# Packed attention scores: the half-seen part moved to the middle columns, and the halves of P swapped

## The chip, the core and the metric

The kernel runs on one core of a Trainium2 chip. The metric is the device time of one launch in microseconds. A core has TensorE (PE, matmuls; its weight loads are shown apart as PEld), VectorE (DVE), ScalarE (ACT), GpSimd (POOL) and SyncE (SP), which run side by side and wait for each other on semaphores. PE writes to PSUM, here eight banks of 128 partitions x 512 f32.

## What is computed

Sliding-window attention with a linear bias, then a two-layer network with a squared relu. Inputs are f32.

```python
batch, n_heads, seq, head_dim = (8, 8, 576, 64)
scores = scale * np.matmul(q, k.transpose(0, 1, 3, 2))
rel = pos[:, None] - pos[None, :]
slopes = 2.0 ** (-8.0 * (np.arange(H, dtype=np.float32) + 1) / H)
bias = slopes[:, None, None] * (-np.abs(rel).astype(np.float32))[None, :, :]
mask = (rel >= 0) & (rel < window)              # window = 128
scores = np.where(mask, scores + bias[None], -1000000000.0)
attn = softmax(scores)                          # with 1e-09 added to the sum
...
x = attn @ v, as 4608 tokens x 512
h = x @ w_in            # 512 -> 2048
r = np.maximum(h, 0.0)
out = (r * r) @ w_out   # 2048 -> 512
```

(The softmax and the last step of attention are put in short form here.)

## The kernel before

**Blocks.** A sequence of 576 is cut in four blocks of 128 queries and one of 64; eight sequences give 40 blocks, numbered m. With a window of 128, a query block sees only its own keys ("part 1") and those of the block before it ("part 0"). The scores are laid out with keys on the partitions and queries along the columns. Of the previous block a query sees only the keys that come after its own place, of its own block only those up to its own place. So, with both blocks cut in half (low = 0 to 63, high = 64 to 127):

| keys (partitions) | previous block, queries low | previous block, queries high | own block, queries low | own block, queries high |
|---|---|---|---|---|
| low | seen in part | never | seen in part | seen in full |
| high | seen in full | seen in part | never | seen in part |

Two of the eight quarters are never seen. Each half of the keys needs three column groups of 64, so 192 columns hold all the scores of a head: two groups mean the same thing for both halves of the keys (previous block with low queries, own block with high queries), and a third means one thing for the low keys (own block, low queries) and another for the high keys (previous block, high queries).

**Packed blocks.** For the blocks with a previous block, 128 queries and m >= 6 (21 of the 40) the function `layout` picks the tag "Pq", and `burst` in `score` (L558 to L583) packs them in this way. Heads come in pairs: index c names a pair, `half` chooses one head of it, and the two heads lie on the lower and the upper 64 rows of PE's array. The output's partitions (low or high keys) choose the columns of the array. So four quarters of the array work at once, each 64 x 64. The list at L564 gives the matmuls of a head, as (part, first key, first query, end of queries, first column):

```python
for part, k0, q0, q1, lo in ((0, 64, 0, 128, 64), (1, 0, 0, 64, 128), (1, 0, 64, 128, 0),
                             (1, 64, 64, 128, 0), (0, 0, 0, 64, 64)):
```

That is five matmuls: high keys 128 + 64 columns, low keys 64 + 64 + 64. In the columns before, 0 to 63 hold the own block with high queries, 64 to 127 the previous block with low queries, and 128 to 191 the group with two meanings.

**After the burst.** ScalarE takes exp of the 192 columns of two heads (of one bank) into the bf16 tile `raw` (L613, four a block). VectorE multiplies by `masks` (the bias's exponential, 0 outside the window) into the tile P (L621): one cut of all 128 partitions and two heads for the two plain groups, four a block, and after every second of these two corner cuts of 64 partitions and four heads for the third group. P holds for each head 256 columns, before the change first the own block's 128 and then the previous block's 128. The two never-seen corners of P are zeroed once, at the start (L395, L396). Then `mix` multiplies P by v (L668), 16 matmuls of 65 columns a block; the 65th column is the sum of the softmax. DVE divides (L691, L696) and the result x is transposed into xT, on PE for 11 blocks and by a DMA transpose on SP (L706) for 29. kqT, the transposed keys and queries, comes in the same way (PE for 9 blocks, SP at L487 for 31).

**Other blocks.** The rest use the tag "P" with whole 64- or 128-column pieces (L579); a block of 64 queries shares a tile with the first block of the next sequence. `at_of` (L541) says where in P each part lies.

**The network.** Tokens go in nine groups g of 512. L772 multiplies xT by w_in (64 matmuls of 512 columns a group, in groups 0 and 1 of fewer columns), ACT takes the relu (L781), DVE squares (L788), and L835 multiplies by w_out.

**The order of the work.** `Plan.order` is a list scheduler. Each `plan.add` gives a task with its engine, its price in ns, a key, the tasks it depends on and the slots that it takes and frees. The planner simulates the engines and DMA rings with these prices, and the resulting start times give the order in which the instructions are written out. Prices thus have no effect but on the order, and, in the first 26 us, on how many filler matmuls on a zero tile (L875) stand in PE's planned gaps. Three prices matter here: `mm(n)`, of nearly every matmul but the score bursts, `max(n, 64) / 2.4 + 1.5`; the score bursts (L584), 220 ns and 176 for each packed unit of four heads; and the masks of L621, `dve(256, 2)` = 205 ns each.

A score burst takes three units (two when it starts early in the list), so a full packed burst has 3 x 2 pairs x 10 = 60 matmuls.

Of the kernel before, what the change touches and what calls it, by code (L numbers as in the profile page):

```python
# [12 lines left out]
ALU = mybir.AluOpType  # L13
# [230 lines left out]
def kernel(  # L244
    ctx: ExitStack, tc: tile.TileContext, q, k, v, moe_w_in, moe_w_out, out
):
    nc = tc.nc
# [41 lines left out]
    ident32 = const.tile([128, 128], FP32)  # L289
    kq32 = const.tile([128, 2, d_model], FP32)  # L290
    zero = const.tile([128, 128], BF16)
    masks = const.tile([128, H, 2, 128], BF16)
    pair_masks = const.tile([128, H, 256], BF16)
    dist = const.tile([128, 2, 128], FP32)
# [14 lines left out]
    raw = ring("raw", size["raw"], [128, H, 256])  # L309
# [8 lines left out]
    def dve(n, rate=1):  # L318
        return n / rate / 0.96 + 72.0

    def mm(n):
        return max(n, 64) / 2.4 + 1.5


    def build_iota():
        nc.gpsimd.iota(dist, pattern=[[128, 2], [1, 128]], base=0, channel_multiplier=-1,
                       allow_small_or_imprecise_dtypes=True)

    t_iota = plan.add({"POOL": 360.0}, -9e5 + 1.005, build_iota)

    def build_ident():
        nc.vector.tensor_single_scalar(ident32, dist[:, 0], 0.0, op=ALU.is_equal)

    t_ident = plan.add({"DVE": 480.0}, -9e5 - 1, build_ident, [t_iota])

# [28 lines left out]
        nc.vector.tensor_copy(pair_masks[:, :, 0:128].rearrange("p h (t s) -> p h t s", t=2), masks[:, :, :, 0:64])  # L364

    def pair_own():
        nc.vector.tensor_copy(pair_masks[:, :, 128:256], masks[:, :, 0, :])

    t_pair = [plan.add({"DVE": n}, PAIR_KEY, f, t_mask) for n, f in ((670.0, pair_rest), (960.0, pair_own))]

# [7 lines left out]
    def zero_task(o, n):  # L378
        def emit():
            nc.vector.memset(o, 0.0)  # L380
        task = plan.add({"DVE": dve(n)}, -9e5 + 9, emit, [t_ones])
        return task
# [9 lines left out]
    zero_first("kqT", kqT, lambda t: t[:, 0:C, 64:128], 128)  # L392
    t_zero_P = []
    for t in Pt["Pq"]:
        t_zero_P.append(zero_task(t[0:64, :, 1, 64:128], 512))  # L395
        t_zero_P.append(zero_task(t[64:128, :, 0, 0:64], 512))  # L396

    def warm():
        idle(bank(sw), WARM)
# [131 lines left out]
    def layout(ms):  # L531
        pair = len(ms) == 2
        quarters = not pair and ms[0] % NKB and blk[ms[0] % NKB] == 128 and ms[0] >= QUARTERS
        sP = Slot("Pq" if quarters else "P")
        work_of = []
        for i, m in enumerate(ms):
            b, kb, n, _, first = where(m)
            parts_of[m] = ([(0, m - 1)] if kb else []) + [(1, m)]
            P_of[m] = (sP, [])
            for part, mk in parts_of[m]:  # L540
                at = 64 * (1 - part) if pair and i == 0 else 128 if pair else 128 * (1 - part)  # L541
                at_of[m, part] = at
                rel = [sk_of[mk]] if part == 0 or kb == NKB - 1 else []
                work_of.append((m, mk, n, at, rel))
        for m in ms:
            P_of[m] = P_of[ms[0]]
        return ms, sP, work_of, where(ms[0])[3]

    def score(units):
# [8 lines left out]
        def burst():  # L558
            for sl in slots.values():
                bank(sl)  # L560
            for (ms, sP, work_of, _), j in units:
                for c in (2 * j, 2 * j + 1) if sP.tag == "Pq" else ():
                    m = ms[0]
                    for part, k0, q0, q1, lo in ((0, 64, 0, 128, 64), (1, 0, 0, 64, 128), (1, 0, 64, 128, 0),  # L564
                                                 (1, 64, 64, 128, 0), (0, 0, 0, 64, 64)):
                        mk = m - 1 + part
                        lo += (c % 2) * 256
                        for half in range(2):
                            rows = slice(half * 64, half * 64 + 64)
                            nc.tensor.matmul(  # L570
                                slots[m, 2 * j + half].tile[k0:k0 + 64, lo:lo + q1 - q0],
                                kqT[sk_of[mk].idx][rows, c, k0:k0 + 64], kqT[sk_of[m].idx][rows, C + c, q0:q1],
                                start=True, stop=True)
                for c in () if sP.tag == "Pq" else (2 * j, 2 * j + 1):
                    for m, mk, w, at, _ in work_of:
                        for k0 in range(0, 128, tall):
                            for half in range(2):
                                rows = slice(half * 64, half * 64 + 64)
                                nc.tensor.matmul(  # L579
                                    slots[ms[0], 2 * j + half].tile.rearrange("p (c x) -> p c x", c=2)[  # L580
                                        k0:k0 + tall, c % 2, at:at + w],
                                    kqT[sk_of[mk].idx][rows, c, k0:k0 + tall], kqT[sk_of[m].idx][rows, C + c, 0:w],
                                    start=True, stop=True)  # L583
# [3 lines left out]
                      [t for u in units for w in u[0][2] for x in w[:2] for t in t_kq_of[x]] + chain["s"],  # L587
                      [*slots.values()] + [u[0][1] for u in first_of if u[0][1].tag == "P"],
                      [x for u in units if u[1] == 1 for w in u[0][2] for x in w[4]])
        tm.n = 4 * sum(5 if u[0][1].tag == "Pq" else len(u[0][2]) * 128 // tall for u in units)  # L590
        plan.bursts.append(tm)
        chain["s"] = [tm]
        for (ms, sP, work_of, due), j in units:
            pair = len(ms) == 2
            hi = max(w[3] for w in work_of) // 128 + 1
            lo = min(w[3] for w in work_of) // 128
            n = 128 if pair else work_of[0][2]
            cols = 2 * sum(w[2] for w in work_of)

            def view(t, pair=pair, lo=lo, hi=hi, n=n):  # L600
                if pair:
                    return t
                return t.rearrange("p c (t q) -> p c t q", t=2)[:, :, lo:hi, 0:n]

            t_exp = []
            for i in (2 * j, 2 * j + 1) if sP.tag == "Pq" else ():
                slot = slots[ms[0], i]
                if i == 0:
                    raw_of[ms[0]] = Slot("raw")
                sr = raw_of[ms[0]]  # L610

                def expo(i=i, slot=slot, sr=sr):
                    nc.scalar.activation(raw[sr.idx][:, 2 * i:2 * i + 2, 0:192],  # L613
                                         slot.tile.rearrange("p (c x) -> p c x", c=2)[:, :, 0:192],
                                         AF.Exp, bias=0.0, scale=scale)
                te = plan.add({"ACT": act(384) + 50.0}, due - 28 + 3 * i, expo, [tm], [sr] if i == 0 else [], [slot])
                t_exp.append(te)

                def mask(ks, hs, lo, to, sr=sr, sP=sP):
                    P = Pt["Pq"][sP.idx].rearrange("p h t q -> p h (t q)")[ks, hs, to]  # L620
                    nc.vector.tensor_tensor(P, raw[sr.idx][ks, hs, lo], masks.rearrange("p h t q -> p h (t q)")[ks, hs, to],  # L621
                                            op=ALU.mult)
                whole, low, high = slice(0, 128), slice(0, 64), slice(64, 128)
                cuts = [(whole, slice(2 * i, 2 * i + 2), whole, slice(64, 192))]
                if i % 2:
                    four, corner = slice(2 * i - 2, 2 * i + 2), slice(128, 192)
                    cuts += [(low, four, corner, low), (high, four, corner, slice(192, 256))]
                for n, w in enumerate(cuts):
                    P_of[ms[0]][1].append(plan.add(
                        {"DVE": dve(256, 2)}, due - 28 + 3 * i, functools.partial(mask, *w),  # L630
                        t_exp[-1:] + t_exp[-2:-1] * (n > 0) + t_zero_P + t_mask,
                        [sP] if i == 0 else [], [sr]))
            for i in () if sP.tag == "Pq" else (2 * j, 2 * j + 1):
                slot = slots[ms[0], i]

                def Pv(i=i, sP=sP, view=view):
                    return view(Pt["P"][sP.idx][:, 2 * i:2 * i + 2].rearrange("p h t q -> p h (t q)"))

                def expo(i=i, Pv=Pv, view=view, slot=slot):
                    nc.scalar.activation(Pv(i), view(slot.tile.rearrange("p (c x) -> p c x", c=2)),  # L640
                                         AF.Exp, bias=0.0, scale=scale)
                te = plan.add({"ACT": act(cols) + 50.0}, due - 28 + 3 * i, expo, [tm], [], [slot])

                def mask(i=i, pair=pair, Pv=Pv, view=view):
                    pt = Pv(i)
                    mk = (pair_masks if pair else masks.rearrange("p h t q -> p h (t q)"))[:, 2 * i:2 * i + 2]
                    nc.vector.tensor_tensor(pt, pt, view(mk), op=ALU.mult)  # L647
                P_of[ms[0]][1].append(plan.add(
                    {"DVE": dve(cols, 2)}, due - 28 + 3 * i, mask,
                    [te] + (t_pair if pair else [t_mask[h] for h in range(H) if place(h) // 2 == i])))  # L650
# [282 lines left out]
```

## Time and profile before

| | |
|---|---|
| median of 7 runs | 312.58 us |
| all runs | 311.9 to 316.07 us |
| the profiled execution | 316.07 us, its span 314.3 us |
| mean granted PE clock | 0.995 |
| PE busy 26 to 80 us | 53.84 of 54.00 us |
| PE busy 244 to 297 us | 53.00 of 53.00 us |
| L613, exp of packed scores | 84 times, mean 501 ns |
| L668, P times v, packed blocks | 336 times, mean 193 ns |
| kqT transposes by DMA | 31, median 6.7 us from issue to landing |
| xT transposes by DMA | 29, median 5.5 us from issue to landing |

How to read the lines that follow. A group's line gives the line of the kernel, the engine, the operation, output <- inputs, the shape (for PE: rows x columns of the array, then rows x streamed columns), the count, then busy time in us and the mean ns of one, then the idle time of the engine ahead of them and who ended it. [...] In a line by stretch come the stretch, its length, and the busy time and count of PE, PEld, DVE, ACT and POOL, then the granted PE clock, the DMA share (here two DMA queues add up, so it can pass 1) and GB/s. A timeline line gives start and length in us; neighbours of one kind are merged.

### The profile page before, as it was taken

Reading aid. Unit: us, or ns where it says so; the run is one execution under the profiler, and the core shown is the slowest. Engines: PE = TensorE matmul, PEld = TensorE weight load, DVE = VectorE, ACT = ScalarE, POOL = GpSimd, SP = SyncE. Lnnn points to the kernel's source line nnn. Section 1 sums busy time; section 2 is a strip of 40 time slices with the busy share of each in tenths; the row PEclk is TensorE's granted clock in tenths of the full one; section 3 lists DMA queues with packets and bytes.
Section 4 is the critical chain, followed back from the end, with each engine's and each line's share of the span. In section 5 each row is a group of like instructions: output and inputs, shape, how many; then the busy total and the mean of one; then the engine's idle time right before and its main releaser. Section 6 shows DMA issues by size and latency. Waiting matters only on the chain.

```text
span 314.3 us, 8213 instructions
## 1 busy us (share of the span) xinstructions
PE 304.0 (97%) x3306; PEld 169.9 (54%) x3306; DVE 170.5 (54%) x563; ACT 171.6 (55%) x338; POOL 107.5 (34%) x134
## 2 busy tenths in 40 slices
PE   7799999999969999999999999999999999999996
PEld 3577887875535455455544554455545454444443
DVE  7774757667345884674736565466547643222200
ACT  4965776574227772774655574367356553434411
POOL 8938577445542527355613333011100000000000
PEclk9999999999997999999999999999999999999999
DMA  9999999999999999999999999998931111000022
GB/s 132 151 184 188 175 185 139 136 136 147 117 123 159 168 132 140 161 94 160 160 219 168 147 158 158 181 136 88 241 111 50 53 52 43 34 35 33 33 88 81
DMA packets 168631, 40.07 MB, mean 127 GB/s; under 512 B 159952, under 2 KB 164304, under 8 KB 168592
## 3 DMA queue, kind: packets, MB, share of 16 engines
q0 software_dynamic: 114896, 18.88, 86.7%
q1 hardware_dynamic: 53696, 20.65, 39.1%
q8 instruction: 26, 0.43, 0.6%
q14 instruction: 13, 0.11, 0.1%
HBM read 36.70 MB, written 9.44 MB: 147 GB/s over the span
## 4 chain that ended last, share of the span: by engine, by line
PE 87%; DMA 7%; POOL 3%; issue 1%; DVE 0%; SPq 0%; ACT 0%; POOLq 0%
PE A L772 39%; PE A L835 38%; PE A L668 5%; DMA w_out_sb<-in_moe_w_out_dram 4%; DMA xT<-x 3%; PE A L570 3%; POOL kq L445 2%; PE A L579 1%; POOL vt L445 1%; PE A L515 1%; PE A L714 1%; POOL w_in_sb L414 0%; SPq L487 0%; ACT kqT L464 0%; DVE Pq L621 0%
## 5 line engine op out<-in xcount | busy, mean ns | idle before, releaser
L772 PE MATMUL A<-xT,w_in_sb 128*128 128x512 bf16 (+3 forms) x768 | 147.1, 327 | 3.1 <-DMA xT<-x 2.9
L835 PE MATMUL A<-w_out_sb,g 128*128 128x512 bf16 (+2 forms) x592 | 147.7, 374 | 0.4 <-DMA w_out_sb<-in_moe_w_out_dram 0.4
L781 ACT ACTIVATE rt<-A 128x512 bf16<-128x512 f32 (+1 forms) x148 | 86.3, 591 | 94.6 <-PE A L772 83.1
L788 DVE TENSOR_TENSOR g<-rt 128x512 bf16<-128x512 bf16 (+1 forms) x148 | 60.9, 415 | 82.9 <-ACT rt L781 82.0
L772 PEld LDWEIGHTS <-w_in_sb 128*128 128x128 bf16 x768 | 68.4, 98 | 53.6 <-issue 3.7
L835 PEld LDWEIGHTS <-g 128*128 128x128 bf16 x592 | 54.2, 98 | 56.2 <-issue 0.9
L445 POOL DMA_DIRECT2D vt<-in_v_dram x40 | 33.9, 850 | 93.3 <-PE A L668 81.6
L621 DVE TENSOR_TENSOR Pq<-raw,masks 64x256 bf16<-64x256 bf16 (+1 forms) x168 | 43.5, 285 | 11.2 <-ACT raw L613 8.3
L445 POOL DMA_DIRECT2D kq<-in_k_dram x39 | 33.7, 864 | 15.8 <-DMA kqT<-kq 7.2
L613 ACT ACTIVATE raw<-A 128x384 bf16<-128x384 f32 x84 | 35.5, 501 | 6.3 <-PE A L570 6.3
L804 ACT ACTIVATE osb<-A 128x512 f32<-128x512 f32 (+1 forms) x36 | 21.5, 598 | 28.3 <-PE A L835 24.5
L445 POOL DMA_DIRECT2D kq<-in_q_dram x39 | 33.6, 861 | 7.0 <-DMA kq<-in_q_dram 2.4
L696 DVE TENSOR_TENSOR x<-A,rec 128x256 bf16<-128x256 f32 (+1 forms) x80 | 32.3, 416 | 0.8
L812 POOL DMA_DIRECT2D out_dram<-osb x3 | 1.7, 564 | 71.9 <-ACT osb L804 71.9
L640 ACT ACTIVATE P<-A 128x512 bf16<-128x512 f32 (+1 forms) x48 | 24.0, 576 | 3.0 <-PE A L579 2.9
L691 DVE RECIPROCAL rec<-A 128x4 f32<-128x4 f32 (+1 forms) x80 | 13.2, 176 | 20.6 <-PE A L668 19.8
L668 PEld LDWEIGHTS <-Pq 128*128 128x128 bf16 x336 | 15.1, 97 | 8.2 <-DVE Pq L621 0.6
L668 PE MATMUL A<-vt,Pq 128*128 128x65 bf16 x336 | 16.6, 193 | 0.2 <-DVE Pq L621 0.2
L668 PEld LDWEIGHTS <-P 128*128 128x128 bf16 x240 | 11.0, 98 | 5.7 <-DVE P L647 0.8
L647 DVE TENSOR_TENSOR P<-P,pair_masks 128x512 bf16<-128x512 bf16 x28 | 11.6, 420 | 3.7 <-ACT P L640 2.7
L570 PEld LDWEIGHTS <-kqT 64*64 64x64 bf16 x840 | 10.0, 110 | 5.6 <-issue 5.5
L668 PE MATMUL A<-vt,P 128*128 128x65 bf16 x240 | 12.1, 193 | 0.7 <-DMA vt<-in_v_dram 0.7
(43 smaller groups left out, 114.2 us busy)
## 6 DMA issues: line engine op xcount, KB each, us to landing
out_dram<-osb SPq DMA_DIRECT2D x32, 256.0 KB, 3.0
vt<-in_v_dram POOLq DMA_DIRECT2D x32, 128.0 KB, 5.7
kq<-in_k_dram POOLq DMA_DIRECT2D x31, 128.0 KB, 7.0
kq<-in_q_dram POOLq DMA_DIRECT2D x31, 128.0 KB, 7.5
w_in_sb<-in_moe_w_in_dram POOLq DMA_DIRECT2D x4, 512.0 KB, 9.0
w_out_sb<-in_moe_w_out_dram POOLq DMA_DIRECT2D x4, 512.0 KB, 10.1
out_dram<-osb POOLq DMA_DIRECT2D x3, 256.0 KB, 2.3
kq<-in_k_dram POOLq DMA_DIRECT2D x8, 64.0 KB, 8.4
```

Source lines behind the costliest of these rows:

```text
L445: nc.gpsimd.dma_start(o, src[b, :, kb * 128:kb * 128 + n, :].rearrange("h s d -> s h d"))
L570: nc.tensor.matmul(slots[m, 2 * j + half].tile[k0:k0 + 64, lo:lo + q1 - q0], kqT[sk_of[mk].idx][rows, c, k0:k0 + 64], kqT[sk_of[m].idx][ro ...
L613: nc.scalar.activation(raw[sr.idx][:, 2 * i:2 * i + 2, 0:192], slot.tile.rearrange("p (c x) -> p c x", c=2)[:, :, 0:192], AF.Exp, bias=0.0 ...
L621: nc.vector.tensor_tensor(P, raw[sr.idx][ks, hs, lo], masks.rearrange("p h t q -> p h (t q)")[ks, hs, to], op=ALU.mult)
L640: nc.scalar.activation(Pv(i), view(slot.tile.rearrange("p (c x) -> p c x", c=2)), AF.Exp, bias=0.0, scale=scale)
L668: nc.tensor.matmul(bank(slot_v)[:, hi * (D + 1):(hi + 1) * (D + 1)], Pt[sP.tag][sP.idx][:, place(h)].rearrange("p t q -> p (t q)")[:, at_o ...
L696: nc.vector.tensor_tensor(xt[sx.idx][0:n, hf * 256:(hf + 1) * 256].rearrange("p (h e) -> p h e", h=4), pv[0:n, :, 0:D], srec.tile[0:n, :]. ...
L772: nc.tensor.matmul(bank(slot)[:, fi * w:(fi + 1) * w], w_in_sb[:, cc, fc * 128:(fc + 1) * 128], xT[:, cc, g * 512 + lo:g * 512 + hi], star ...
L781: nc.scalar.activation(srt.tile[:, 0:cols], slot.tile[:, 0:cols], AF.Relu, bias=0.0, scale=1.0)
L788: nc.vector.tensor_tensor(sg.tile[:, fcs[0]:fcs[-1] + 1, lo:hi], r, r, op=ALU.mult)
L804: nc.scalar.activation(so.tile[:, lo:hi], slot.tile[:, lo:hi], AF.Copy)
L835: nc.tensor.matmul(bank(slot)[:, lo:hi], sg.tile[:, fc, t * 128:(t + 1) * 128], w_out_sb[:, fc, lo:hi], start=fc == 0, stop=fc == FCB - 1)
```

## The change

The list of matmuls has four entries. The group with two meanings moves to columns 64 to 127. With it in the middle, "own block, low queries" and "own block, high queries" are neighbours for the low keys, as the two groups of the previous block are for the high keys, so one matmul of 128 columns writes both. For that the halves of P and of `masks` are swapped: previous block first, own block second. The two plain groups are now columns 0 to 63 and 128 to 191 of `raw`, and columns 0 to 63 and 192 to 255 of P and `masks`, so the wide mask cut has two runs of 64 for each head. The mask source `dist` starts at 128 and falls, the identity and one pair mask are taken from its other half, and the zeroed corners move along. In the planner, `mm` is 0.8 ns a matmul higher, and the masks cost 205 ns (wide) and 290 ns (corners); the count of instructions in a burst goes from 5 to 4 a head. The price of a burst stays.

```diff
     def mm(n):
-        return max(n, 64) / 2.4 + 1.5
+        return max(n, 64) / 2.4 + 2.3
...
-        nc.gpsimd.iota(dist, pattern=[[128, 2], [1, 128]], base=0, channel_multiplier=-1,
+        nc.gpsimd.iota(dist, pattern=[[-128, 2], [1, 128]], base=128, channel_multiplier=-1,
...
-        nc.vector.tensor_single_scalar(ident32, dist[:, 0], 0.0, op=ALU.is_equal)
+        nc.vector.tensor_single_scalar(ident32, dist[:, 1], 0.0, op=ALU.is_equal)
...
-        nc.vector.tensor_copy(pair_masks[:, :, 128:256], masks[:, :, 0, :])
+        nc.vector.tensor_copy(pair_masks[:, :, 128:256], masks[:, :, 1, :])
...
-        t_zero_P.append(zero_task(t[0:64, :, 1, 64:128], 512))
-        t_zero_P.append(zero_task(t[64:128, :, 0, 0:64], 512))
+        t_zero_P.append(zero_task(t[0:64, :, 0, 64:128], 512))
+        t_zero_P.append(zero_task(t[64:128, :, 1, 0:64], 512))
...
-                at = 64 * (1 - part) if pair and i == 0 else 128 if pair else 128 * (1 - part)
+                at = 64 * part if pair and i == 0 else 128 * part
...
-                    for part, k0, q0, q1, lo in ((0, 64, 0, 128, 64), (1, 0, 0, 64, 128), (1, 0, 64, 128, 0),
-                                                 (1, 64, 64, 128, 0), (0, 0, 0, 64, 64)):
+                    for part, k0, q0, q1, lo in ((0, 64, 0, 128, 0), (1, 0, 0, 128, 64),
+                                                 (1, 64, 64, 128, 128), (0, 0, 0, 64, 0)):
...
-        tm.n = 4 * sum(5 if u[0][1].tag == "Pq" else len(u[0][2]) * 128 // tall for u in units)
+        tm.n = 4 * sum(4 if u[0][1].tag == "Pq" else len(u[0][2]) * 128 // tall for u in units)
...
                 def mask(ks, hs, lo, to, sr=sr, sP=sP):
-                    P = Pt["Pq"][sP.idx].rearrange("p h t q -> p h (t q)")[ks, hs, to]
-                    nc.vector.tensor_tensor(P, raw[sr.idx][ks, hs, lo], masks.rearrange("p h t q -> p h (t q)")[ks, hs, to],
-                                            op=ALU.mult)
-                whole, low, high = slice(0, 128), slice(0, 64), slice(64, 128)
-                cuts = [(whole, slice(2 * i, 2 * i + 2), whole, slice(64, 192))]
+                    P = Pt["Pq"][sP.idx].rearrange("p h t q -> p h (t q)")[ks, hs]
+                    mk = masks.rearrange("p h t q -> p h (t q)")[ks, hs]
+                    r = raw[sr.idx][ks, hs]
+                    if to is None:
+                        o, r, mk = (t.rearrange("p h (a b) -> p h a b", b=64)[:, :, 0:n:n - 1]
+                                    for t, n in ((P, 4), (r[:, :, 0:192], 3), (mk, 4)))
+                    else:
+                        o, r, mk = P[:, :, to], r[:, :, lo], mk[:, :, to]
+                    nc.vector.tensor_tensor(o, r, mk, op=ALU.mult)
+                low, high = slice(0, 64), slice(64, 128)
+                cuts = [(slice(0, 128), slice(2 * i, 2 * i + 2), None, None)]
                 if i % 2:
-                    four, corner = slice(2 * i - 2, 2 * i + 2), slice(128, 192)
-                    cuts += [(low, four, corner, low), (high, four, corner, slice(192, 256))]
+                    cuts += [(ks, slice(2 * i - 2, 2 * i + 2), high, to)
+                             for ks, to in ((low, slice(128, 192)), (high, high))]
...
-                        {"DVE": dve(256, 2)}, due - 28 + 3 * i, functools.partial(mask, *w),
+                        {"DVE": 205.0 if n == 0 else 290.0}, due - 28 + 3 * i, functools.partial(mask, *w),
```

More of the change, by code (lines that the diff above doesn't have):

```diff
@@ L594, in score @@
             pair = len(ms) == 2
-            hi = max(w[3] for w in work_of) // 128 + 1
             lo = min(w[3] for w in work_of) // 128
@@ L598, in score, with view @@
             cols = 2 * sum(w[2] for w in work_of)
-            def view(t, pair=pair, lo=lo, hi=hi, n=n):
+            def view(t, pair=pair, lo=lo, n=n):
                 if pair:
                     return t
-                return t.rearrange("p c (t q) -> p c t q", t=2)[:, :, lo:hi, 0:n]
+                return t.rearrange("p c (t q) -> p c t q", t=2)[:, :, lo:2, 0:n]
             t_exp = []
```

## The prediction

> **What bounds the kernel now.** I read the page's busy times first, then the chain that ended last, then busy time by stretch, then the waits, and last the one kind of burst that the change rewrites.
>
> ```profile
> PE 304.0 (97%) x3306; PEld 169.9 (54%) x3306; DVE 170.5 (54%) x563; ACT 171.6 (55%) x338; POOL 107.5 (34%) x134
> ...
> PE 87%; DMA 7%; POOL 3%; issue 1%; DVE 0%; SPq 0%; ACT 0%; POOLq 0%
> ```
>
> TensorE (PE) is busy for 304.0 of 314.3 us and carries 87% of the chain; VectorE (DVE) carries none of it. So time is won by giving PE less to do, or lost by making PE wait. The stretches say where it still waits (us; PE, PEld, DVE, ACT, POOL busy; granted clock):
>
> ```profile
> 0.00:26.00 26.00, 21.92 (x241) 14.62 (x242) 18.57 (x64) 16.95 (x37) 19.01 (x28) 1.00 1.53 160
> 26.00:80.00 54.00, 53.84 (x826) 41.22 (x824) 36.34 (x124) 34.22 (x71) 34.04 (x41) 1.00 1.95 155
> 80.00:90.00 10.00, 9.73 (x129) 5.10 (x127) 4.70 (x17) 3.71 (x8) 4.69 (x6) 1.00 2.12 127
> 90.00:98.00 8.00, 5.06 (x81) 2.44 (x78) 2.35 (x7) 2.69 (x6) 2.32 (x3) 0.79 1.92 130
> 98.00:170.00 72.00, 71.94 (x838) 36.91 (x837) 47.45 (x165) 45.30 (x90) 32.31 (x39) 1.00 1.80 159
> 170.00:244.00 74.00, 74.00 (x821) 37.30 (x820) 41.60 (x133) 41.35 (x81) 13.47 (x17) 1.00 1.02 138
> ```
>
> PE misses 4 us in the first 26, then nothing but one hole near 90 us. The waits name the hole:
>
> ```profile
> PE A L772 <- DMA xT<-x: 2.9, 1, 2.9
> ```
>
> One transposed tile of x landed at 92.9 us; PE waited, and its clock fell to 0.79 in that stretch. The start-to-start times of single matmuls there put the gap at 3.1 us and the slower matmuls after it at another 1.4 us or so. The profiled run took 316.07 us (span 314.3 and 1.8 around it). Without that hole it would be 316.07 - 4.5 = 311.6; the other six runs took 311.9 to 313.1. So the median run, 312.58, has at most about 1 us of this kind of wait, and I take the hole as mostly a property of the profiled run.
>
> Now the burst, groups by form and then the timeline of the burst at 136.65 us:
>
> ```profile
> L570 PE MATMUL A<-kqT 64*64 64x64 bf16 x504 | 11.2, 196 | 0.0
> L570 PE MATMUL A<-kqT,kqT 64*64 64x128 bf16 x168 | 10.5, 226 | 0.0
> L570 PE MATMUL A<-kqT,kqT 64*64 64x64 bf16 x168 | 10.2, 195 | 0.0
> L570 PEld LDWEIGHTS <-kqT 64*64 64x64 bf16 x840 | 10.0, 110 | 5.6 <-issue 5.5
> ```
> ```profile
> 136.74 0.24 PE L570 MATMUL A<-kqT,kqT 64*64 64x64 bf16 x4
> ...
> 136.84 0.23 PE L570 MATMUL A<-kqT,kqT 64*64 64x64 bf16 x4
> ...
> 136.93 0.23 PE L570 MATMUL A<-kqT,kqT 64*64 64x64 bf16 x4
> ...
> 137.36 0.39 PE L772 MATMUL A<-xT,w_in_sb 128*128 128x512 bf16 x1
> ```
>
> 840 matmuls are 21 packed blocks x 8 heads x 5. A full burst is 60 of them (6 pairs of heads, one head on each half of the array's rows). The rows "kqT,kqT 64x64" recur once a pair: 136.74, .84, .93, that is every 95 ns. In the timeline's records the burst starts at 136.652, its last matmul starts 580 ns later, the next L772 starts 125 ns after that; the L772 before it started 309 ns ahead of the burst, where two such matmuls are 216 ns apart. So a burst costs 93 + 705 = 798 ns, of which 93 and about 96 are the changes of shape at its ends, which stay.
>
> **The change part by part.**
>
> *Fewer matmuls.* 21 x 8 = 168 matmuls and their 168 weight loads go. The columns streamed don't: each half of the keys still gets 192 columns a head (before 128+64 on the high half and 64+64+64 on the low; after 128+64 on both). The single starts show what a matmul costs in its quarter of the array. Low keys: starts every 31 to 32 ns, three of them 95 ns. High keys: 59 ns after the 128-column one and 28 or 29 after the 64-column one, together 87.5. The low half with its three matmuls sets the pace; 192 columns cost 95 ns in three pieces, 87.5 in two. After the change both halves have the two-piece form, which the high half shows today, so a pair takes 87.5 ns: 7.5 x 84 pairs (21 x 4) = 0.63 us, all on PE's path. Bounds: if the new pairing doesn't reach 87.5 because both 128-column pieces now start together, the gain is 0; if the burst is paced by instructions instead (580/60 = 9.7 ns each), it is 168 x 9.7 = 1.6 us. I take 0.63, since each half's own spacing is seen directly.
>
> [...]
>
> *The wide mask cut (L621, 84 times).* It becomes two runs of 64 elements a head where it was one of 128. Today's two forms bracket it:
>
> ```profile
> L621 DVE TENSOR_TENSOR Pq<-raw,masks 64x256 bf16<-64x256 bf16 x84 | 23.7, 282 | 0.7
> L621 DVE TENSOR_TENSOR Pq<-raw,masks 128x256 bf16<-128x256 bf16 x84 | 23.0, 288 | 10.5 <-ACT raw L613 8.3
> ```
>
> By the code the first has four runs of 64 and the second two of 128; 282 and 288 ns say that shorter runs cost nothing. I take 0. [...] DVE is half idle, so what counts is how long P is ready before PE takes it. Over the 21 blocks the starts of the P matmuls lie behind the end of the masks they need by 0.06 and 0.26 us for the first four heads in the tightest two blocks, by 0.17, 0.42 and 0.44 us for the last four in the tightest three, and by 0.6 to 12.5 us in the rest. [...]
>
> *The corner cuts, zeros, iota, identity, pair masks.* Same counts and sizes at other columns: 0. The cover is that they are set-up in the first 26 us, or the same 282 ns step. ScalarE's exponentials read the same 192 columns: 0.
>
> *The planner's prices.* Every matmul is priced 0.8 ns higher (2.3 where it was 1.5 over columns/2.4), the two corner masks 290 where they were 205. The trace says that both are nearer the truth: a 512-column matmul comes every 216 ns (planned 214.8, now 215.6), and from one corner to the next corner DVE takes 288 to 291 ns. No instruction gets longer by it, but the list of all 3306 matmuls is laid out anew: by 90 us the plan is some 1080 x 0.8 = 0.9 us later, and near ties fall otherwise. Steps moved by it are the P matmuls, the x transposes on SP and the loads on POOL. What such a move can cost is bounded by the trace: at best the ~1 us of waiting in the median and part of the 4 us missing in the first 26 us; at worst one more hole like the one at 90 us, 4.5 us. I take 0, since after 98 us PE has no hole, and most xT tiles land 0.8 to 2.3 us before their first matmul, where a local shift over 10 us (46 matmuls x 0.8) is 0.04 us.
>
> Sum: on the profiled run's own time 316.07 - 0.63 = 315.4; on the median of the runs 312.58 - 0.63 = 312.0 (rounded).
>
> **The rivals.** About 0.5% (1.6 us) is what a measurement of this kernel can tell from no change: bounds 311.0 and 314.1.
>
> *Slower: the new order makes PE wait for an xT tile in every run.* At 68 to 90 us the transposes on SP take 7 to 9 us from issue to landing, and two issues held SP itself for 4.8 and 6.7 us; the tile that PE waited for had no slack. For it: that stage is already at its limit, and a kqT transpose put ahead of an xT one on SP is enough. Against it: the six other runs show at most 1 us. It decides once the tile lands over 2 us behind its matmul (2.2 in place of 0.63 gained, clock loss included). Price: the profiled run's excess, 3.5 us: 312.0 + 3.5 = 315.5.
>
> *Faster than the sum: the plan that agrees with the chip removes waits.* The remaining 1 us of xT wait and some 0.6 of the 4 us at the start go: 312.0 - 1.6 = 310.4. For it: both new prices match the trace. Against it: PE is full from 26 us on but for the hole.
>
> [...]
>
> *The change doesn't shorten the burst:* the columns are the same 192 a half; 312.6.
>
> **How the numbers follow.** Likeliest, the sum: 0.45, 311.2 to 313.0 by itself. No shorter burst, or slower masks: 0.10, within 0.5%. Faster rival: 0.21. Slower rival: 0.24. Of the sum's 0.45, 0.03 falls below 311.0 with the burst's upper bound (1.6 us), and 0.02 above 314.1 with part of a hole. Faster 0.24, same 0.50, slower 0.26. The range reaches into both rivals, 310.3 to 315.0.
>
> **What the profile after would show.** L570 with 672 matmuls, 336 of them 128 columns wide; full bursts of 48, with pairs every 87 to 88 ns and about 660 ns from first matmul to the next shape instead of 705. [...] PE busy from 98 us to 297 us without holes. The prediction is wrong if PE shows a new wait for DMA xT, kqT or vt, or if the first 26 us miss clearly more or less than 4 us of PE.

## The result and the profile after

The changed kernel takes 310.71 us (median of 27 runs) against 312.59 us (64 runs of the kernel before beside it): ratio 0.9939, 95% interval 0.9925 to 0.9953, so 1.9 us less (1.5 to 2.3). The forecast was 312.0 us, 0.6 us less, in a range of 310.3 to 315.0. The changed kernel's profiled execution took 310.01 us, with a span of 308.3.

The page's busy times, and busy time by stretch (columns as before):

```profile
PE 300.9 (98%) x3138; PEld 167.9 (54%) x3138; DVE 170.6 (55%) x563; ACT 170.9 (55%) x338; POOL 107.6 (35%) x134
```
```profile
0.00:26.00 26.00, 22.06 (x245) 14.85 (x246) 18.44 (x64) 17.37 (x38) 19.41 (x28) 1.00 1.57 163
26.00:80.00 54.00, 54.00 (x786) 41.02 (x785) 36.17 (x123) 33.60 (x70) 33.51 (x41) 1.00 2.02 157
80.00:90.00 10.00, 9.44 (x114) 4.85 (x113) 5.00 (x18) 3.71 (x8) 5.77 (x8) 1.00 2.01 136
90.00:98.00 8.00, 8.00 (x118) 4.34 (x117) 5.46 (x20) 6.27 (x13) 4.11 (x6) 1.00 2.37 153
98.00:170.00 72.00, 72.00 (x770) 36.42 (x769) 46.53 (x155) 43.42 (x85) 31.53 (x38) 1.00 1.79 161
```

168 matmuls are gone, PE is full from 26 us to 297 us but for 0.56 us ahead of 90 us, and the start misses 3.9 us as before. The 0.56 us are a wait for a tile of xT:

```profile
PE A L777 <- DMA xT<-x: 0.6, 1, 0.6
```

The burst is as forecast. By form, and in the timeline of the burst at 135.12 us (rows kept: the first matmuls of a pair, and the ends):

```profile
L570 PE MATMUL A<-kqT 64*64 64x128 bf16 x168 | 10.1, 222 | 0.0
L570 PE MATMUL A<-kqT,kqT 64*64 64x128 bf16 x168 | 10.1, 223 | 0.0
L570 PEld LDWEIGHTS <-kqT 64*64 64x64 bf16 x672 | 8.6, 108 | 5.9 <-issue 5.9
```
```profile
135.12 0.24 PE L570 MATMUL A<-kqT,kqT 64*64 64x128 bf16 x2
...
135.30 0.24 PE L570 MATMUL A<-kqT,kqT 64*64 64x64 bf16 x4
...
135.38 0.24 PE L570 MATMUL A<-kqT,kqT 64*64 64x64 bf16 x4
135.41 0.24 PE L570 MATMUL A<-kqT 64*64 64x128 bf16 x4
135.47 0.24 PE L570 MATMUL A<-kqT,kqT 64*64 64x64 bf16 x4
...
135.77 0.39 PE L777 MATMUL A<-xT,w_in_sb 128*128 128x512 bf16 x1
```

336 matmuls are 128 columns wide. The single matmuls overlap (one of 128 columns is shown with 222 ns); their starts give a pair every 87.5 ns (one and the same matmul of the six pairs starts 86, 174, 261, 349, 436 and 524 ns behind the burst's first), and 649 ns from the burst's first matmul to the next L777, where it was 705 in the burst shown before. The wide mask cut, now with two runs of 64, has not changed:

```profile
L627 DVE TENSOR_TENSOR Pq<-raw,masks 64x256 bf16<-64x256 bf16 x84 | 23.7, 282 | 0.8
L627 DVE TENSOR_TENSOR Pq<-raw,masks 128x256 bf16<-128x256 bf16 x84 | 22.4, 288 | 12.4 <-ACT raw L612 10.5
```

So 56 ns in each of 14 bursts (84 pairs, six to a burst) explain about 0.8 us. Where do the other 1.1 us come from? My first theory was the order that the new planner prices give.

### The profile page after: what moved, and what is told of

The parts are those of the page before. It is cut to its first block, busy times and chain, and to the rows that moved or that the text cites. A ratio compares the mean times of both kernels' runs of the same rounds, so it can differ in the third digit from the quotient of the medians.

```text
span 308.3 us, 7879 instructions
## 1 busy us (share of the span) xinstructions
PE 300.9 (98%) x3138; PEld 167.9 (54%) x3138; DVE 170.6 (55%) x563; ACT 170.9 (55%) x338; POOL 107.6 (35%) x134
## 4 chain that ended last, share of the span: by engine, by line
PE 89%; DMA 6%; POOL 3%; issue 0%; DVE 0%; POOLq 0%
PE A L777 40%; PE A L840 39%; PE A L673 5%; DMA w_out_sb<-in_moe_w_out_dram 4%; PE A L570 3%; DMA xT<-x 3%; POOL kq L445 2%; PE A L579 1%; POOL vt L445 1%; PE A L515 1%; PE A L719 1%; POOL w_in_sb L414 0%; POOL dist L326 0%; DVE osb L811 0%; POOLq L326 0%
## 5 line engine op out<-in xcount | busy, mean ns | idle before, releaser
L777 PE MATMUL A<-xT,w_in_sb 128*128 128x512 bf16 (+3 forms) x768 | 145.3, 326 | 0.8 <-DMA xT<-x 0.6
L777 PEld LDWEIGHTS <-w_in_sb 128*128 128x128 bf16 x768 | 68.5, 98 | 51.6 <-DMA w_in_sb<-in_moe_w_in_dram 0.7
L570 PEld LDWEIGHTS <-kqT 64*64 64x64 bf16 x672 | 8.6, 108 | 5.9 <-issue 5.9
```

The lines of the kernel that those rows point to most:

```text
L570: nc.tensor.matmul(slots[m, 2 * j + half].tile[k0:k0 + 64, lo:lo + q1 - q0], kqT[sk_of[mk].idx][rows, c, k0:k0 + 64], kqT[sk_of[m].idx][ro ...
L777: nc.tensor.matmul(bank(slot)[:, fi * w:(fi + 1) * w], w_in_sb[:, cc, fc * 128:(fc + 1) * 128], xT[:, cc, g * 512 + lo:g * 512 + hi], star ...
```

## Experiments

### The two halves of the change apart

**four_old_order**: the changed kernel with the old prices, so that every instruction outside the bursts stands in the order of before.

```diff
-        return max(n, 64) / 2.4 + 2.3
+        return max(n, 64) / 2.4 + 1.5
-        tm.n = 4 * sum(4 if u[0][1].tag == "Pq" else ...
+        tm.n = 4 * sum(5 if u[0][1].tag == "Pq" else ...
-                        {"DVE": 205.0 if n == 0 else 290.0}, ...
+                        {"DVE": dve(256, 2)}, ...
```

> Four matmuls a head and the swapped halves of P, but the planner's prices of before, so every instruction outside the bursts stands in the order of before. Theory (the burst gives 56 ns each in 14 bursts, about 0.8 us; the rest of the 1.9 us came from the order that the new prices give): 311.8 us, ratio 0.9975. Rival (the shorter burst brings all of it, since what follows it starts earlier): 310.7 us, ratio 0.994.

Measured: 310.42 us, ratio 0.9935 (0.9915 to 0.9956).

**five_new_order**: the kernel before with the new prices, the same three edits the other way round.

> The kernel before with the new prices alone (0.8 ns more a matmul, masks at 205 and 290 ns, four instructions a head counted): five matmuls a head in the order of the changed kernel. Theory (order worth 1.1 us): 311.5 us, ratio 0.9965. Rival (the burst brings all): 312.6 us, ratio 1.000.

Measured: 312.10 us, ratio 0.9982 (0.9964 to 0.9999). The theory falls: with the old order the four matmuls bring all of the gain, and the new order brings some 0.2% (0.36% at most by the interval).

**four_mm15**: the changed kernel with the old matmul price alone, a third order (`+ 2.3` to `+ 1.5`).

> The changed kernel with the matmul price of before (1.5 ns over columns/2.4), masks at 205 and 290 ns: a third order. If the nearer matmul price is what made the order better, this loses the 1.1 us: 311.8 us. If the mask price did it, 310.7 us. If it is chance which order has the waits, anything from 310.5 to 313.

Measured: 310.80 us, ratio 0.9946 (0.9931 to 0.9961). Three orders of the four-matmul kernel lie within 0.4 us. For the four-matmul kernel the prices are worth nothing that these runs can tell.

**six_new_order**: what paces a burst.

```diff
-((0, 64, 0, 128, 0), (1, 0, 0, 128, 64), (1, 64, 64, 128, 128), (0, 0, 0, 64, 0))
+((0, 64, 0, 64, 0), (1, 0, 0, 64, 64), (0, 64, 64, 128, 64), (1, 0, 64, 128, 128),
+ (1, 64, 64, 128, 128), (0, 0, 0, 64, 0))
```

> The changed kernel with both 128-column matmuls of a head cut in two, so six matmuls of 64 columns, three on each half of the keys; same prices, same order. If the fullest quarter of the array sets the pace, a pair takes 95 ns as with five matmuls, and the time is 0.8 us over the changed kernel: 311.5 us. If the number of instructions sets the pace (a pair took 95 ns with 10, 88 with 8), a pair takes 105 to 115 ns and the time is 1.5 to 2.3 us over the changed kernel: 312.2 to 313.0 us.

Measured: 312.44 us, ratio 0.9984 (0.9967 to 1.0002), so some 1.4 us over the changed kernel, between the two forecasts. The single starts of the burst at 137.02 us tell why: the second to the fifth pair begin every 95 ns (116, 211, 306, 401 ns behind the first), as three 64-column matmuls one behind the other took before (95 ns), but the sixth begins 141 ns behind the fifth; it is 634 ns from first to last start against 527. From the second to the fifth pair the pace is the quarter's; why the sixth comes later, these runs don't tell. (The profile also waits 1.0 us longer for an xT tile near 90 us than the changed kernel's, so it is not shown that the bursts, 14 times 0.107 us by this estimate, are all of the 1.4 us.)

### Where the excess lies

Four matmuls gain 1.3 to 2.0 us in two orders, and the bursts account for 0.8. New theory: PE waits less for DMA.

**five_light** and **four_light**: the kernel before, and four_old_order, with half the rows of most loads left out, so that the DMA queues have less to do and the order stays. (The rows left out hold older data, so what these two compute is no longer the attention.)

```diff
+                w = 64 if m >= 7 and m != 10 else n
-                o = (vt[sl.idx][0:n, :, 0:D] if nm == "v"
-                     else kq[sl.idx][0:n, i].rearrange("s (h d) -> s h d", h=H))
+                o = (vt[sl.idx][0:w, :, 0:D] if nm == "v"
+                     else kq[sl.idx][0:w, i].rearrange("s (h d) -> s h d", h=H))
-  ... src[b, :, kb * 128:kb * 128 + n, :] ...
+  ... src[b, :, kb * 128:kb * 128 + w, :] ...
```

> The kernel before, but for blocks from 7 on (all but block 10) only the first 64 of 128 rows of k, q and v are loaded, so those DMAs move half the bytes; the order of instructions stays. The rest of the rows hold older data. It is a pair with four_light. If the excess of the measured 1.9 us over the 0.8 us of the shorter bursts is DMA waits of PE ahead of 110 us, they vanish here: about 311.0 us, and the pair differs by 0.8 us. If the excess lies elsewhere on PE, the pair differs by 1.7 to 2.0 us.

> Four matmuls a head in the order of before (four_old_order), with the same halved loads as five_light. Excess in DMA waits: 0.8 us below five_light, about 310.2 us. Excess on PE itself: 1.7 to 2.0 us below five_light.

Measured: five_light 310.96 us, ratio 0.9949 (0.9929 to 0.9970); four_light 310.31 us, ratio 0.9928 (0.9908 to 0.9949). With light queues the pair differs by 0.65 us, close to what the bursts are worth. four_light is no faster than four_old_order (310.42), five_light is 1.5 us faster than the kernel before: the excess is a wait of the five-matmul kernel that the four-matmul kernel in this order mostly lacks, and that goes with the load on the DMA queues.

**before_look** and **before_look2**: two more profiles of the kernel before, no edit.

> The kernel before once more, for a second profile. If its usual time has DMA waits, PE shows one or more holes between 60 and 110 us that add up to about 1 us, and from the burst near 103 us to the end it takes 206.0 + 0.8 us. If the excess is on PE, the stretch from that burst to the end takes over 207.5 us.

> As before_look, a third profile of the kernel before: the same expectation, to see whether the holes stand at one place.

Measured: 312.25 and 312.53 us, usual times. From the burst at 102.8 us to the end they take 207.7 and 208.0 us, which by what I had written puts the excess on PE and not on data. Behind the first 26 us the waits of before_look2 name no DMA, but a hole ended by "issue", the profile's word for time in which the engine waited for nothing that it shows:

```profile
PE A L579 <- issue: 1.2, 1, 1.2
```

The timelines of before_look and before_look2 show it, inside one burst:

```profile
109.40 0.20 PE L579 MATMUL A<-kqT,kqT 64*64 64x64 bf16 x4
109.43 0.25 PE L579 MATMUL A<-kqT 64*64 64x64 bf16 x5
110.57 0.25 PE L579 MATMUL A<-kqT 64*64 64x128 bf16 x3 [0.89 <-issue]
```
```profile
109.43 0.25 PE L579 MATMUL A<-kqT 64*64 64x64 bf16 x5
110.85 0.25 PE L579 MATMUL A<-kqT 64*64 64x128 bf16 x3 [1.17 <-issue]
```

Both stop three matmuls ahead of the end of the burst. Counted by weight loads (each with its matmul, and PE's few waits and drains), both stop after PE's instruction 3009, and the profiled run of before had a gap of 0.3 us at 114.1 us after the same one. The page lists a DMA queue of kind "instruction":

```profile
q8 instruction: 26, 0.43, 0.6%
```

That is 26 packets of 16 KB beside PE's 6,631 instructions, 255 to a packet if the queue carries PE's, and the positions at which PE stops (below) lie 256 instructions or a multiple of that apart. So I take a packet to be a piece of 256 instructions of PE, an estimate from these counts. Packet times and positions, from the trace, in us:

```
kernel                packet near 108 us   burst begins   stops after   goes on
before_look           107.80 to 109.05     108.82         3009          110.57
before_look2          108.09 to 109.30     108.82         3009          110.85
before, profiled run  111.73 to 113.02     113.51         3009          114.43
five_new_order        109.04 to 110.36     109.33         3009          111.84
four_old_order        111.90 to 113.57     108.61         no stop       -
changed kernel        111.14 to 112.68     108.63         no stop       -
```

The packet in the table is the one that follows the piece ending at 3009. In the four traces that stop it began with 132 to 156 instructions left. Among 512-column matmuls (216 ns each) 130 instructions, 65 matmuls with their weight loads, last 14 us. A burst of 68 matmuls is 136 instructions and uses them up in 0.65 us, while PE went on only 2.7 to 2.8 us after the packet began (107.80 to 110.57). In these four the packet began 0.3 to 1.8 us ahead of the burst, and PE stood for 0.3 us (before, profiled run), 0.9 and 1.2 us (before_look, before_look2) and 1.5 us (five_new_order).

How many are left is not fixed. In before_look the packets between 47 and 110 us, with the DMA queues busy, begin with 99 to 153 left; from 250 us on, with the queues nearly idle, with 280 to 290. In five_light, with light queues and the same instructions, the packet for 3009 began at 105.79 us with 184 left and ended at 106.82, 2.2 us ahead of the burst, and PE runs through 3009. That fits the excess going with the DMA load: under load the packet came later.

The other stops fit. four_old_order stops for 0.3 us at 66.8 us and four_mm15 for 0.6 us at 67.4 us, both after instruction 1729 or 1730, five times 256 ahead of 3009; before_look for 0.3 us at 57.4 us and five_light for 0.6 us at 57.6 us, both after 1473, six times 256 ahead. So the four-matmul kernel has such stops too, but smaller ones.

One matmul in five dropped from each packed head shifts the boundary. By the burst near 109 us, four_old_order has had 136 fewer instructions (its burst begins at 2743, not 2879), and the piece that ends at 3009 ends well behind that burst (PE reaches 3009 only at 117.0 us).

### Testing the fetch theory

**five_shift30** and **four_shift140**: more instructions at the very start. The warm-up's 2560 columns of a zero tile are cut in more matmuls: 20 and 75 in place of 5.

```diff
-        idle(bank(sw), WARM)
+        for w in [128] * 20:                   # four_shift140: [32] * 70 + [64] * 5
+            nc.tensor.matmul(bank(sw)[:, 0:w], zero, zero[:, 0:w], start=True, stop=True)
```

> The kernel before with its 20 x 128 warm-up columns in 20 matmuls in place of 5: 30 more instructions ahead of everything, the same columns and the same order after. New theory: the excess over the 0.8 us is one hole of PE in the burst near 109 us, where PE runs through the last instructions of a 16 KB fetch (256 instructions) before the next fetch has come, and 30 instructions more move that fetch some 20 matmuls ahead of the burst. Then the hole goes and the time is 311.2 to 311.5 us, ratio 0.9965. Rival (DMA waits for data by chance, whatever the instruction count): 312.5 us, ratio 1.000.

> Four matmuls a head in the order of before, with the warm-up's 2560 columns in 75 matmuls in place of 5: 140 more instructions. By the fetch theory the end of a fetched piece now falls two instructions ahead of the end of the 128-instruction burst near 109 us, and its fetch starts just ahead of that burst: a hole of 1 to 1.5 us appears there, 311.4 to 312.2 us against 310.4 of four_old_order. Rival (the four-matmul burst lost the hole by being shorter, or waits are by chance): 310.4 us.

Measured: five_shift30 312.62 us, ratio 0.9998 (0.9980 to 1.0016); four_shift140 311.04 us, ratio 0.9951 (0.9929 to 0.9973). In five_shift30 the hole near 109 us is gone as forecast (the burst runs through), but the time is not: a wait of 1.1 us for an xT tile stands at 90 us.

```profile
89.72 0.41 PE L672 MATMUL A<-vt,P 128*128 128x65 bf16 x8
91.26 0.81 PE L776 MATMUL A<-xT,w_in_sb 128*128 128x512 bf16 x3 [1.14 <-DMA xT<-x]
```

The tile landed at 91.1 us, against 89.4 and 89.7 in before_look and before_look2. An instruction packet ran from 87.90 to 89.37 in this run, and only from 89.3 on in those two; whether it held up the tile is not shown. In four_shift140 the fetch began at 107.41 us, 1.6 us ahead of the burst at 109.02 and not just ahead of it, and the burst lost only 0.1 us at instruction 3009, which PE reached 1.15 us behind the packet's end. The 0.6 us over four_old_order stand in the first 33 us (0.8 us later there). The hole was placed wrongly, and the run does not decide whether a full one comes back.

**five_split** and **four_hole**: the same test, with the added instructions between the xT wait near 90 us and the burst near 109 us. Matmuls of token group 2, of the second and third of the four steps of the sum, are cut in 2 or 4 pieces.

```diff
+                    cut = {2: 4, 3: 4, 4: 2, 5: 2}.get(fc, 1) if g == 2 and cc in (1, 2) else 1
+                    # four_hole: 4 for fc 1 to 10, 2 for 11 and 12
+                    for a in range(0, w, w // cut):
+                        z = a + w // cut
-   nc.tensor.matmul(bank(slot)[:, fi * w:(fi + 1) * w], ..., xT[:, cc, g * 512 + lo:g * 512 + hi], ...)
+   nc.tensor.matmul(bank(slot)[:, fi * w + a:fi * w + z], ..., xT[:, cc, g * 512 + lo + a:g * 512 + lo + z], ...)
```

> The kernel before, with 8 of the 512-column matmuls of token group 2 (93 to 107 us) cut in pieces: 32 more instructions between the xT wait near 90 us and the burst near 109 us, 0.03 us more of PE, and every other instruction in the same order. Fetch theory: the end of the fetched piece now falls 98 instructions into that burst of 136 and its fetch starts some 40 instructions ahead of it, so the hole of 1.1 to 1.4 us goes, while the xT wait near 90 us, ahead of the edit, stays as before: 311.2 to 311.5 us, ratio 0.996 to 0.9965. Rival (another wait takes the hole's place, as with the 30 instructions at the start): 312.5 us, ratio 1.000.

> Four matmuls a head in the order of before, with 22 pairs of matmuls of the same token group cut in pieces: 128 more instructions ahead of the burst near 109 us, 0.2 us more of PE. Fetch theory: the fetch starts at the first instruction of that burst of 128, and 138 instructions are at hand, gone in about 0.8 us, so PE stands for 1.5 to 2 us behind the burst: 312.0 to 312.6 us, ratio 0.9985 to 1.000. Rival (with four matmuls there is no such hole): 310.6 us, ratio 0.994.

Measured: five_split 311.89 us, ratio 0.9976 (0.9957 to 0.9995); four_hole 312.06 us, ratio 0.9979 (0.9963 to 0.9994).

four_hole is the clear one: the hole is back, at the place that was set for it, with four matmuls a head. Its packet ran from 107.27 to 108.92, the burst began at 108.03, and PE stopped after instruction 3009:

```profile
108.62 0.26 PE L579 MATMUL A<-kqT 64*64 64x64 bf16 x8
108.82 0.33 PE L673 MATMUL A<-vt,Pq 128*128 128x65 bf16 x5
110.46 0.27 PE L673 MATMUL A<-vt,Pq 128*128 128x65 bf16 x3 [1.32 <-issue]
```

From one start to the next that is 1.51 us, 1.48 more than usual. With 0.2 us for the cut matmuls it makes 1.7; measured are 1.6 us over four_old_order by the medians, 1.4 by the ratios.

five_split won half of what I had expected, 0.6 of 1.2 us. In its profile PE runs through instruction 3009. But the burst near 109 us now stops for 0.55 us at another place, for a kqT tile, and a later wait for an xT tile appears:

```profile
109.63 0.25 PE L579 MATMUL A<-kqT 64*64 64x128 bf16 x4 [0.38 <-DMA kqT<-kq]
...
117.88 0.59 PE L838 MATMUL A<-w_out_sb,g 128*128 128x512 bf16 x2
119.70 0.81 PE L775 MATMUL A<-xT,w_in_sb 128*128 128x512 bf16 x3 [1.23 <-DMA xT<-x]
```

That execution took 313.0 us, more than the median, so these waits may not be in every run. But the second is of the kind that five_shift30 has too: with the hole gone, the next thing that is late is a tile from a DMA transpose.

## Why the prediction was right, and what it missed

**Direction and range** held, and the likeliest case's mechanism, the shorter burst, is real; but its size is a third of what came. By itself that case was to give 311.2 to 313.0 us, and 310.71 lies below. The range held the result because it reached down to the faster rival's end, 310.3, and that rival's reason did not hold. So that part of being right is luck.

**Fewer matmuls, 0.63 us.** Right: a pair takes 87.5 ns, as the high half's own spacing said. The bursts gain a little more than the term. From the burst near 126 us to the end, the same order takes 184.37 us in before_look and 183.87 in four_old_order; 48 pairs lie there, so 10.4 ns a pair. Burst by burst, from its first matmul to the one behind it and with the stops left out, the changed kernel's 18 bursts are 0.81 us shorter in all than those of before_look. The last pair of a five-matmul burst was slower than 95 ns (112 in one at 132.8 us), which I had not counted. The upper bound of 9.7 ns for each removed instruction, 1.6 us, was not it. A weight load is shown with 110 ns, yet in the kernel before three matmuls with theirs passed in 95 ns.

**The wide cut, 0.** Right: 288 ns before and after; no run shows the slower masks that the chances allow for.

**The planner's prices, 0.** About right in size: 0.9982 (0.9964 to 0.9999) with five matmuls, some 0.6 us, and no difference that can be told among three orders with four. The rival that had the new prices remove waits came near the measured time for a wrong reason.

**The step that missed: "I take 0, since after 98 us PE has no hole", and that at most about 1 us of the median is waiting "of this kind".** It rested on one execution. That one had lost 3.1 us at 90 us, so its burst near 113 us came 1.8 us after the fetch had begun, and the stop after instruction 3009 cost 0.3 us over the usual spacing. In two usual executions the same stop costs 1.1 to 1.4 us. It was in the trace of before that the forecast used, as a gap of 0.3 us inside a burst, and the "instruction" queue stood in the page. The missing term is PE's instruction supply: I counted the removed instructions by what they cost in the array, not by how they move the fetch boundary against the bursts. Sum for the pair with one order, before_look to four_old_order (spans 310.48 and 308.63): 0.21 us up to the burst near 109, 1.14 from it to the next, 0.50 after; 1.85 in all. About 0.8 of it is the shorter bursts, 1.1 the hole, less 0.1 for other waits of the start (four_old_order waits 0.5 us for a tile of w_in at 28 us and stops at 66.8 us, before_look stops at 57.4 us).

**The slower rival** (a wait for xT in every run) came in a small form. The changed kernel's profile has the wait for DMA xT that the forecast named as a sign of being wrong, 0.56 us ahead of 90 us; before_look and before_look2 have none there. All four profiles with any of the new prices have one near 90 us (five_new_order 0.7 us, four_mm15 1.3, six_new_order 1.6). Yet the changed kernel's median is only 0.3 us over that of four_old_order, whose profile has none, and their intervals overlap, so a cost in every run is not shown. five_shift30 and five_split, in the old order, show that such a wait lies close by there too.

**What stays open.** That the hole comes with the instruction count is shown by four_hole, and that it goes, by five_shift30 and five_split; five_light shows that it also goes when the same packet comes earlier. That the time of the five-matmul kernel would follow in full was not shown: waits for transposed tiles took the place of all of it in five_shift30 and about half in five_split. Why a tile is late there, whether by the moved instruction packets or by PE being earlier, was not settled. How often and how large the hole is over all executions is known from the profiled ones alone.

## What to carry to other kernels

Count the instructions that an edit removes twice: by their time on the engine, and by where they put the boundaries of the instruction fetch against dense bursts, since the stop at 3009 cost more here (1.1 to 1.5 us in before_look, before_look2 and four_hole, where the packet began 0.7 to 1.0 us ahead of the burst) than the removed instructions did (0.8 us). In four_hole, 128 more instructions with the same columns brought the stop back. A gap that ends on "issue" inside a burst, at the same instruction number in several executions, was the sign here. (Count by weight loads: four_old_order also shows ten gaps of 0.2 us on "issue" behind bursts, but there the trace lacks matmul records, 3096 of them beside 3138 weight loads.) Take two or three profiles of the kernel before where the forecast is below 1%: the one with the longest time hid here what the usual ones wait for.

## What the runs showed of the hardware

The queue of kind "instruction" that fits PE's count has packets of 16,384 bytes, 26 in the trace of before beside 6,631 instructions of PE and 24 in the changed kernel's beside 6,296. PE's stops of this kind stand at positions that differ by a multiple of 256: 3009 (five executions of three kernels, and 0.1 us in four_shift140), 1729 or 1730 (two) and 1473 (two). PE went on 1.4 to 1.6 us after the packet's end at 3009 in those five, and 1.3 to 1.6 us after it at the smaller stops. In the 14 traces PE reached the end of a piece less than 1.3 us behind the next packet's end at eleven places, and stopped for 0.1 to 1.6 us at ten of them. At nearly all of the 24 to 27 packets of an execution PE did not stop; at 3009, behind a burst of some 130 instructions in 0.65 us, the stop cost 1.1 us in before_look, 1.4 in before_look2 and 1.5 in four_hole.

On quarters of 64 x 64 three 64-column matmuls one behind the other took 95 ns and a 128-column with a 64-column one 87.5 ns, for the same 192 columns, so 7.5 ns for the third piece. With three pieces on all four quarters (six_new_order) the 95 ns held for the second to the fifth pair of heads, and then the pace broke.
